# The first unit's second product in Strassen form, and all sums of the second weights made in one stage

## The chip, the cores and the metric

The kernel runs on one core of a Trainium2 chip. The metric is the device time of one execution in microseconds (us). The core has a matrix engine (TensorE, "PE" in the profile, its weight loads "PEld"), VectorE ("DVE"), ScalarE ("ACT"), GpSimd ("POOL"), and SyncE ("SP"), which here only issues transfers. Each engine works through its own list of instructions in order, and waits at an instruction until what it needs has been signalled by the others.

## The reference

Attention over chunks of 64 tokens, then a layer norm and a two-layer FFN with a residual:

```python
scores = scale * np.matmul(q_c, k_c.transpose(0, 1, 2, 4, 3))   # 8 x 8 heads, chunks of 64, D = 64
attn = softmax(scores)                                          # max subtracted
x = np.matmul(attn, v_c)                                        # -> (8, 576, 512) = 4608 tokens x 512
xn = (x - mu) / np.sqrt(var + 1e-06) * g_ln
ch = np.maximum(xn @ w_ch1, 0.0) @ w_ch2                        # 512 -> 2048 -> 512
return x + ch
```

All of it is float32. The kernel gets that accuracy from the matrix engine's faster float32 format by splitting each operand into a high and a low part and adding three products: high by high, high by low, low by high.

## The kernel before

The 4608 tokens are nine tiles of 512, each of two pairs of 256. The first three tiles (numbers 0, 1 and 2) go through the FFN in the plain way: for each of 16 blocks `f` of 128 hidden features, `up(f)` is 12 matmuls into one of two PSUM banks called `h` (line L565), `split(f)` makes the high part `hh` on ScalarE (L578) and the low part `hl` on VectorE (L579), and `down(f)` is 12 matmuls into the four banks `y` (L589): eight that read `hh`, then four that read `hl`. A bank `h` is free again when `hl` has been made.

The other six tiles form three units of two tiles (1024 tokens). In a unit both products can go by a Strassen scheme: seven products of half the size in each direction, on sums of the operand's quarters, in place of eight. The first product does so in all units (`product`, L1049, 336 matmuls of 512 columns). The second does so in units 1 and 2 (class `double`, L960, 672 matmuls of 256 columns each); in unit 0 it is plain (L1175, 384 matmuls of 512 columns). The weights stream from DRAM through a ring of six buffers.

The Strassen form needs sums of the second weights' quarters, in high and low parts, for eight pairs `p` of 128-row blocks. `mix` makes one of the eight: two adds of 128x512 (L992), four additions or subtractions of 128x256 (L999), one cast of 128x1024 on ScalarE (L1002), two subtractions of 128x512 (L1005), and two writes of 512 KB into the DRAM tensor `wb` (L1009, L1010). `mix_early` does it from the weights that are still in the local memory, during the third tile's FFN: numbers 4, 5 and 6 on GpSimd, number 7 on VectorE from the end of that stage into unit 0. `mix_late` does numbers 0 to 3 on VectorE at the end of unit 0, from ring buffers.

While the FFN of one tile or unit runs, the attention of later ones runs beside it. Its matmuls are scores (`s`, L309) and attention by values (L409). In most pairs the latter writes two banks `h`, the same two that `up` uses; VectorE then divides out of both (L443) and frees them. Between the two, a turned copy of the probabilities is made, on VectorE (`STREAM_TRANSPOSE`, L380) or on the matrix engine (L358, L368).

The order of all this is written by hand. For the first three tiles it is a table of letters per step (`START`, `SECOND`, `THIRD`): each letter advances one generator by one `yield`, ahead of the FFN's step of that number. In `THIRD`, which belongs to the third tile's FFN (number 2), `C`, `D`, `G`, `H` are attention, `S` writes the first weights' sums, `T`, `V`, `W` are the mixing of numbers 4 and 5, 6, and 7, and `P`, `Q` are `combine`, which makes unit 0's operands `xc` (casts on ScalarE L798, differences `rows` on VectorE L805, low parts on GpSimd L802). For units, `BEGINS`, `PAIR_STEPS`, `HALVES` give the counts of matmuls at which the next unit's generators advance. SyncE's list follows the same order, so a transfer there waits behind every one that was written ahead of it.

Of the kernel before, what the change touches and what calls it, by code (L numbers as in the profile page):

```python
# [17 lines left out]
P = 128  # L18
# [33 lines left out]
BEGINS = ((8, 122, 236, 350), (4, 92, 154, 246))  # L52
STEPS = (0, 5, 9, 14, 20, 31, 42, 53, 61, 67, 72, 77, 85, 90, 97, 104, 116, 128, 140)
ACROSS = (0, 5, 9, 14, 20, 31, 42, 53, 61, 67, 72, 77, 110, 116, 123, 130, 142, 154, 166)
# [28 lines left out]
FAST = 1  # L83
# [24 lines left out]
def chunk_attention_ffn(ctx: ExitStack, tc: tile.TileContext, qkv, v01, g, w, out):  # L108
# [598 lines left out]
    class Ring:  # L707
# [313 lines left out]
    def mix_late(i):  # L1021
        first = ring.passed + 4 * i

        def parts_of(k):
            w = ring.at(first + k)[:, : 2 * DM].rearrange("p (h n) -> p h n", h=2).bitcast(F32)
            return w[:, 0], w[:, 1]

        return mix(i, shared[f"h{2 * i}"][:, 0], shared[f"h{2 * i + 1}"][:, 0].bitcast(F32R), parts_of, nc.vector)

    def unit_ffn(u):  # L1030
        first = 2 * LEAD + 4 * u
        fast = u >= FAST
# [48 lines left out]
        plan = double(u, hu, mix_2, mix_3, mix_4) if fast else None  # L1081

        more = []
        order = [(n, f) for n in range(2) for f in order_of(u, n)]
        parts = []

        def split(i):
            n, f = order[i]
            if i % 5 > 1:
                hh, hl = more[i % 5 - 2][:, 0], more[i % 5 - 2][:, 1]  # L1090
            else:
                hh, hl = (hp_.tile([P, 1, DM], F32R, name=f"h{c}")[:, 0] for c in "hl")
            x = hu[f // 2][:, n, f % 2]
            nc.scalar.activation(hh, x, AF.Relu)
            parts.append((hh, hl, x))

        def rest(i):
            hh, hl, x = parts[i]
            nc.vector.scalar_tensor_tensor(
                out=hl, in0=x, scalar=0.0, in1=hh.bitcast(F32), op0=ALU.max, op1=ALU.subtract  # L1100
            )

        for q in range(NF // 4):
# [25 lines left out]
            for e in range(2):  # L1129
                steps += [  # L1130
                    (a_, e, "4", lambda e: nc.scalar.activation(h[e][:, 0, 1], a_[e], AF.Relu if fast else AF.Copy))
                ]
            for i, (bank, e, name, then) in enumerate(steps):
                if i % 2 == 0:
                    w01 = pair_of()
                product(bank[e], w01[i % 2], name, name in "215")
                yield 6
                if i % 2:
                    ring.fetch()
                if then:  # L1140
                    then(e)
                if fast:
                    if name == "7":
                        waiting.append((14 * q + i + 2, h[e][:, 1, 1]))
                    if waiting and waiting[0][0] <= 14 * q + i:
                        relu(waiting.pop(0)[1])
                    if q > 0 and i in (4, 6):
                        mix_1(2 * (q - 1) + i // 2 - 2)
                    if q == NF // 4 - 1:
                        plan.advance((i + 1 - len(steps)) * 0.945)  # L1150
                    if q == NF // 4 - 1 and i in (12, 13):
                        mix_1(2 * q + i - 12)
                    continue
                if q == NF // 4 - 1 and name in "73":
                    (split if name == "7" else rest)(e)
                if q == NF // 4 - 1 and name == "4":
                    if e == 0:
                        for n, g in ((2, "raw"), (1, "wf")):
                            x = raws.tile([P, n, 2, DM], F32R, name="hx", tag=g)
                            more.extend(x[:, i] for i in range(n))  # L1160
                    (rest if e else split)(2)

        if fast:
            assert not waiting
            yield from plan.products()
            return
# [180 lines left out]
```

## Time and profile before

| | us |
|---|---|
| median of three runs (lowest, highest) | 831.44 (830.99, 833.67) |
| the profiled execution | 830.98 |
| its span, first to last instruction | 829.2 |
| busy: TensorE / VectorE / ScalarE / GpSimd | 819.8 / 602.8 / 326.8 / 174.3 |
| unit 0 (from its first matmul to unit 1's) | 325.7 to 499.5 |
| unit 1 | 499.5 to 668.6 |

A row of the timeline has the start, the length, the engine, the line, the operation, its output and inputs, the number of instructions that are merged in it, and in brackets how long its engine sat idle ahead of it and who ended that. A merged row's length runs from the first start to the last end. In the chain of waits a row has start, length and the engine's work. In a table of stages each engine has its busy time and in brackets its number of instructions.

### The profile page before, as it was taken

What the parts mean: (1) busy time and instruction counts of PE and PEld (TensorE: products, weight loads), DVE (VectorE), ACT (ScalarE), POOL (GpSimd) and SP (SyncE); (2) the same over time, 40 slices, a digit from 0 to 9 for tenths busy, and PEclk for the clock granted to TensorE, in tenths of its full rate; (3) what the DMA queues carried; (4) which work ended last, traced back from release to release, by engine and by line L of the source; (5) the groups of instructions that cost most, each with busy time, mean ns of one, the idle gap of its engine ahead of it and who ended that gap; (6) DMA issues with size and microseconds to landing.
All of it is one profiled execution on the core that took longest, in us unless ns stands there. A gap on an engine that the chain in (4) does not pass through costs nothing.

```text
span 829.2 us, 16241 instructions
## 1 busy us (share of the span) xinstructions
PE 819.8 (99%) x6442; PEld 701.1 (85%) x6442; DVE 602.8 (73%) x983; ACT 326.8 (39%) x513; POOL 174.3 (21%) x156
## 2 busy tenths in 40 slices
PE   7999999999999999999999999999999999999998
PEld 5898888888888887888888888888999988889998
DVE  6998966787655956876787866797889953248954
ACT  4776431132332332323324433434544632354432
POOL 0110006463855754000005101000002700000000
PEclk9999999999999999999999999999999999999999
DMA  9998416958784336978877999787796686668662
GB/s 360 331 279 238 157 47 222 344 172 291 282 294 125 128 136 254 326 223 301 266 245 214 347 300 346 263 262 249 246 308 211 181 285 196 195 190 286 212 209 104
DMA packets 105531, 199.53 MB, mean 241 GB/s; under 512 B 8816, under 2 KB 61552, under 8 KB 103536
## 3 DMA queue, kind: packets, MB, share of 16 engines
q1 hardware_dynamic: 103008, 191.68, 68.0%
q0 software_dynamic: 2448, 6.82, 4.4%
q8 instruction: 51, 0.84, 0.4%
q14 instruction: 24, 0.20, 0.1%
HBM read 140.79 MB, written 48.76 MB: 229 GB/s over the span
## 4 chain that ended last, share of the span: by engine, by line
PE 98%; DMA 1%; DVE 0%; SPq 0%; issue 0%; ACT 0%; DVEq 0%
PE y L1049 28%; PE y L960 19%; PE h L565 16%; PE y L589 16%; PE y L1175 8%; PE h L1175 3%; PE s L309 2%; PE h L409 1%; DMA k_t<-qkv 1%; PE s L409 1%; PE s L358 1%; PE s L335 0%; PE y L249 0%; PE s L497 0%; PE y L518 0%; PE s L518 0%
## 5 line engine op out<-in xcount | busy, mean ns | idle before, releaser
L1049 PE MATMUL y<-xc,ring 128*128 128x512 f32 x1008 | 233.7, 391 | 0.0
L1049 PEld LDWEIGHTS y<-xc,ring 128*128 128x128 f32 x1008 | 187.9, 188 | 39.5
L565 PE MATMUL h<-xth,wp 128*128 128x512 f32 (+1 forms) x432 | 129.5, 370 | 0.0
L960 PE MATMUL y<-ring,hx 128*128 128x256 f32 x876 | 108.5, 283 | 0.0
L960 PEld LDWEIGHTS y<-ring,hx 128*128 128x128 f32 x876 | 106.6, 192 | 0.0
L1058 DVE TENSOR_TENSOR hu<-y,snap 128x512 f32<-128x512 f32 x72 | 49.1, 687 | 67.1 <-ACT snap L1055 35.0
L589 PE MATMUL y<-wp,hh 128*128 128x512 f32 x376 | 96.2, 394 | 0.0
L565 PEld LDWEIGHTS h<-xth,wp 128*128 128x128 f32 x432 | 78.2, 188 | 14.4 <-DVE hl L579 0.5
L589 PEld LDWEIGHTS y<-wp,hh 128*128 128x128 f32 x376 | 69.1, 188 | 13.9
L579 DVE SCALAR_TENSOR_TENSOR hl<-h,hh 128x512 fp32r<-128x512 f32 (+1 forms) x53 | 33.1, 629 | 62.4 <-ACT hh L578 62.0
L565 PE MATMUL h<-xtl,wp 128*128 128x512 f32 (+1 forms) x216 | 78.3, 367 | 0.0
L1055 ACT COPY snap<-y 128x512 f32<-128x512 f32 x72 | 42.0, 586 | 79.2 <-PE y L1049 79.2
L578 ACT ACTIVATE hh<-h 128x512 fp32r<-128x512 f32 (+1 forms) x53 | 28.7, 546 | 105.7 <-PE h L565 105.7
L380 DVE STREAM_TRANSPOSE pt_sb<-p_sb 32x256 f32<-32x256 f32 x144 | 62.7, 436 | 4.6 <-ACT p_sb L344 2.3
L802 POOL TENSOR_TENSOR xc<-rows,xc 128x512 fp32r<-128x512 f32 x28 | 49.8, 1788 | 73.8 <-ACT xc L798 72.2
L897 ACT ACTIVATE hx<-hu 128x512 fp32r<-128x512 f32 x73 | 45.3, 630 | 49.1 <-PE y L960 44.3
L906 DVE TENSOR_TENSOR hx<-hu,hx 128x512 fp32r<-128x512 f32 x62 | 45.3, 740 | 11.6 <-ACT hx L897 10.9
L459 POOL TENSOR_TENSOR rstd<-vare,mhalf 128x2 f32<-128x2 f32 x12 | 11.1, 927 | 194.8 <-DVE vare L458 194.8
L589 PE MATMUL y<-wp,hl 128*128 128x512 f32 x188 | 51.8, 390 | 0.0
L565 PEld LDWEIGHTS h<-xtl,wp 128*128 128x128 f32 x216 | 40.3, 188 | 6.6 <-ACT xtl L528 0.2
L960 PE MATMUL y<-ring,hh 128*128 128x256 f32 x312 | 45.2, 283 | 0.0
L1175 PE MATMUL y<-ring,hx 128*128 128x512 f32 x162 | 42.2, 390 | 0.0
(168 smaller groups left out, 1197.2 us busy)
## 6 DMA issues: line engine op xcount, KB each, us to landing
ring<-wa SPq DMA_DIRECT2D x84, 512.0 KB, 4.6
ring<-w2d SPq DMA_DIRECT2D x56, 512.0 KB, 5.0
ring<-wb SPq DMA_DIRECT2D x32, 512.0 KB, 4.0
raw<-w SPq DMA_DIRECT2D x15, 1024.0 KB, 8.0
out<-x SPq DMA_DIRECT2D x18, 512.0 KB, 5.3
q_t<-qkv SPq DMA_DIRECT2D x17, 512.0 KB, 5.8
k_t<-qkv SPq DMA_DIRECT2D x17, 512.0 KB, 6.7
v_t<-qkv SPq DMA_DIRECT2D x32, 256.0 KB, 6.1
```

The source lines that it names most:

```text
L380: nc.vector.transpose(out=pt_sb[quad(2 * h2 + j), :, c, quad(i)], in_=p_sb[quad(2 * c + i), :, h2, quad(j)])
L565: nc.tensor.matmul(h, lhsT=(wh, wh, wl)[m][:, ks], rhs=(xth, xtl, xth)[m][:, k, :], start=i == 0, stop=i == len(terms) - 1,)
L579: nc.vector.scalar_tensor_tensor(out=hl, in0=h, scalar=0.0, in1=hh.bitcast(F32), op0=ALU.max, op1=ALU.subtract)
L589: nc.tensor.matmul(sums(pairs[j // 2])[j % 2], lhsT=(hh, hh, hl)[m], rhs=(wh, wl, wh)[m], start=f == 0 and m == 0, stop=f == NF - 1 and m ...
L802: engine.tensor_tensor(out=o[:, 1], in0=x, in1=o[:, 0].bitcast(F32), op=ALU.subtract)
L897: nc.scalar.activation(hh, self.split[i][2], AF.Relu if x == "1" else AF.Copy)
L906: nc.vector.tensor_tensor(out=hl, in0=x, in1=hh.bitcast(F32), op=ALU.subtract)
L960: nc.tensor.matmul(bank[j // 2][:, j % 2 * PAIR : (j % 2 + 1) * PAIR], lhsT=(hh, hh, hl)[m][:, j * P : (j + 1) * P], rhs=loaded[t // 2][:, ...
L1049: nc.tensor.matmul(bank, lhsT=w[:, (0, 0, 1)[m], ks], rhs=x[:, (0, 1, 0)[m], k, :], start=start and k == m == 0, stop=k == 1 and m == 2, s ...
L1055: nc.scalar.copy(out, bank)
L1058: nc.vector.tensor_tensor(out=out, in0=bank, in1=s, op=ALU.add)
L1175: nc.tensor.matmul(ys[j], lhsT=(hh, hh, hl)[m], rhs=w[:, (0, 1, 0)[m]], start=f == 0 and m == 0, stop=f == NF - 1 and m == 2,)
```

## The change

Unit 0's second product takes the Strassen form too, so that all units have one plan; the plain code, its table entries and `mix_late` go. The sums of the second weights must then all be in DRAM by unit 0's second product. All eight are made in the third tile's stage: 4, 5, 6 on GpSimd as before, and 1, 2, 3, 7 and 0 on VectorE. Numbers 1, 2, 3 and 7 are made from the weights in local memory, in the places `w1`, `w2`, `w3`, `w8`; number 0's weights have gone by then, and are read back from DRAM into `w9` (`mix_again`).

```diff
 THIRD = {
-    ... 6: "DGS", 7: "GGHSTT", 8: "DGTT", 9: "D", 10: "GGPT",
+    ... 6: "DGSaa", 7: "GGHSTTaa", 8: "DGTTabb", 9: "Daaabb", 10: "GGPTcc", ...
...
-BEGINS = ((8, 122, 236, 350), (4, 92, 154, 246))
+BEGINS = (4, 92, 154, 246)
...
-PAIR_STEPS = ((STEPS, STEPS, ACROSS, STEPS), (STEPS, BY_TENSOR, WIDE, AT_END))
-HALVES = (((426, 8), (562, 12)), ((512, 8), (612, 10)))
+PAIR_STEPS = (STEPS, BY_TENSOR, WIDE, AT_END)
+HALVES = ((512, 8), (612, 10))
...
-            ring.loads.extend(w2d[f][:, :, :] for n in range(2) for f in order_of(u, n))
-            continue
...
-    def mix_late(i):
...
-        return mix(i, shared[f"h{2 * i}"][:, 0], shared[f"h{2 * i + 1}"][:, 0].bitcast(F32R), parts_of, nc.vector)
+    def mix_again(tag, p):
+        t_ = const.tile([P, 2, 2, DM], F32, name="mixed", tag=tag)
+        for k in range(2):
+            nc.sync.dma_start(t_[:, :, k], w2d[2 * p + k])
+        yield
+        yield from mix(
+            p, t_[:, 0], t_[:, 1].bitcast(F32R), lambda k: [t_[:, 0, k], t_[:, 1, k]], nc.vector
+        )
...
-        plan = double(u, hu, mix_2, mix_3, mix_4) if fast else None
+        plan = double(u, hu, mix_2, mix_3, mix_4)
...
-                nc.scalar.copy(staged[:, jj], ys[j])
-                nc.gpsimd.dma_start(spilled[pair][:, jj], staged[:, jj], accum_op=ALU.add)
...
-            V=mix_early(const, "w7", (6,), nc.gpsimd), W=mix_early(const, "w12", (7,), nc.vector), ...
+            V=mix_early(const, "w7", (6,), nc.gpsimd), W=mix_early(const, "w8", (7,), nc.vector), ...
+            a=mix_early(const, "w1", (1,), nc.vector), b=mix_early(const, "w2", (2,), nc.vector), c=mix_early(const, "w3", (3,), nc.vector),
+            d=mix_again("w9", 0), P=combine(0, 0), Q=combine(0, 1),
...
-                by_pe = len(PAIR_STEPS[u - 1][n]) == len(BY_TENSOR)
+                by_pe = len(PAIR_STEPS[n]) == len(BY_TENSOR)
...
-        side = [(at, now["Q"]) for at in REST] + [(at, now["W"]) for at in LAST_MIXED]
+        side = [(at, now["Q"]) for at in REST]
```

The lines of the changed file are numbered lower: L579 becomes L574, L443 L438, L409 L404, L992 L975, L999 L982, L1005 L988, L960 L943, L724 L719.

VectorE's list in the third tile, from the low part of block 5 to the attention division of the pair on letter `G`. Before:

```order
L579 SCALAR_TENSOR_TENSOR hl<-h,hh 128x512 x2
L380 STREAM_TRANSPOSE pt_sb<-p_sb 32x8x32 x16
L579 SCALAR_TENSOR_TENSOR hl<-h,hh 128x512
L387 TENSOR_REDUCE den<-p_sb 128x16
L388 TENSOR_SCALAR den<-den 128x16
L389 RECIPROCAL rden<-den 128x16
L443 TENSOR_TENSOR x<-h,rden 128x8x64 x2
```

The first row holds the low parts of blocks 4 and 5, the third that of block 6. In the changed kernel the same stretch, from the end of number 2's (`b`) quarters on, reads:

```order
L982 TENSOR_TENSOR mixed<-mixed 128x256 x4
L574 SCALAR_TENSOR_TENSOR hl<-h,hh 128x512
L375 STREAM_TRANSPOSE pt_sb<-p_sb 32x8x32 x8
L975 TENSOR_TENSOR mixed<-wp 128x512 x2
L375 STREAM_TRANSPOSE pt_sb<-p_sb 32x8x32 x8
L982 TENSOR_TENSOR mixed<-mixed 128x256 x4
L574 SCALAR_TENSOR_TENSOR hl<-h,hh 128x512
L382 TENSOR_REDUCE den<-p_sb 128x16
L383 TENSOR_SCALAR den<-den 128x16
L384 RECIPROCAL rden<-den 128x16
L988 TENSOR_TENSOR mixed<-mixed 128x512 x2
L438 TENSOR_TENSOR x<-h,rden 128x8x64 x2
```

Between the low parts of blocks 5 and 6 now stand number 3's (`c`) two adds and four quarter operations, and ahead of the division number 2's two subtractions.

SyncE's list from the end of the third tile into unit 0. Before:

```order
L1009 DMA wb<-mixed 128x1024
L1010 DMA wb<-mixed 128x1024
L724 DMA ring<-wa 128x1024 x2
L268 DMA x<-out 128x2x512 x2
L281 DMA q_t<-qkv 128x1024
L281 DMA k_t<-qkv 128x1024
L724 DMA ring<-wa 128x1024 x4
L612 DMA out<-x 128x512 x4
```

In the changed kernel:

```order
L719 DMA ring<-wa 128x1024 x2
L992 DMA wb<-mixed 128x1024
L993 DMA wb<-mixed 128x1024
L263 DMA x<-out 128x2x512 x2
L276 DMA q_t<-qkv 128x1024
L276 DMA k_t<-qkv 128x1024
L719 DMA ring<-wa 128x1024 x4
L992 DMA wb<-mixed 128x1024
L993 DMA wb<-mixed 128x1024
L607 DMA out<-x 128x512 x4
```

Number 7's writes now stand ahead of the loads of `x` (the third tile's residual), of the next pair's q and k, and of four ring buffers; number 0's stand behind them.

TensorE's list at the start of unit 0. Before:

```order
L1049 MATMUL y<-xc,ring 128x512 x12
L309 MATMUL s<-k_t,q_t 64x64 x32
L1049 MATMUL y<-xc,ring 128x512 x66
L409 MATMUL h<-v_t,pt_sb 64x64 x32
L1049 MATMUL y<-xc,ring 128x512 x48
```

In the changed kernel:

```order
L1031 MATMUL y<-xc,ring 128x512 x6
L304 MATMUL s<-k_t,q_t 64x64 x32
L1031 MATMUL y<-xc,ring 128x512 x66
L404 MATMUL h<-v_t,pt_sb 64x64 x32
L1031 MATMUL y<-xc,ring 128x512 x24
L304 MATMUL s<-k_t,q_t 64x64 x32
L1031 MATMUL y<-xc,ring 128x512 x30
L363 MATMUL s<-ident,p_sb 128x128 x8
```

The scores come six matmuls earlier, the next pair's follow sooner, and two of the four pairs are turned on the matrix engine (L363), as in unit 1 before. Within the third tile TensorE's list is the same as before.

More of the change, by code (lines that the diff above doesn't have):

```diff
@@ L82 @@
 LONG = 40
-FAST = 1
 def layout(room, side, tail=False):
@@ L1154, in unit_ffn @@
[L1154 to L1166, printed above, removed]
@@ new lines, in unit_ffn @@
+                if name == "7":
+                    waiting.append((14 * q + i + 2, h[e][:, 1, 1]))
+                if waiting and waiting[0][0] <= 14 * q + i:
+                    relu(waiting.pop(0)[1])
+                if q > 0 and i in (4, 6):
+                    mix_1(2 * (q - 1) + i // 2 - 2)
+                if q == NF // 4 - 1:
+                    plan.advance((i + 1 - len(steps)) * 0.945)
+                    if i in (12, 13):
+                        mix_1(2 * q + i - 12)
+        assert not waiting
@@ L1220, in weave @@
+        yield from plan.products()
     def weave(ffn, side):
@@ L1287, in chunk_attention_ffn @@
         now["N"] = following(1, 0)
-        now.update(zip("u1", tiles[2].ffn(0, 2, room=ROOMS[2])), X=bring(range(2 * LEAD - 2, 2 * LEAD)))
+        now.update(zip("u1", tiles[2].ffn(0, 2, room=ROOMS[2])))
         play(layout(ROOMS[2], THIRD, True), now)
-        side = [(at, now["Q"]) for at in REST] + [(at, now["W"]) for at in LAST_MIXED]
+        side = [(at, now["Q"]) for at in REST]
         for u in range(UNITS):
@@ L1293, in chunk_attention_ffn @@
                 for n in range(4):
-                    begin, steps = BEGINS[u][n], PAIR_STEPS[u][n]
+                    begin, steps = BEGINS[n], PAIR_STEPS[n]
                     side += [(begin + at, following(u + 1, n)) for at in steps]
                     side.append((begin + steps[0], following(u + 1, n + 1)))
-                for half, (begin, step) in enumerate(HALVES[u]):
+                for half, (begin, step) in enumerate(HALVES):
                     stream = combine(u + 1, half)
                     side += [(begin + i * step, stream) for i in range(13)]
-            if u + 1 == FAST:
-                starts = {}
-                def late(i):
-                    if i not in starts:
-                        starts[i] = mix_late(i)
-                    next(starts[i])
-                for i in range(NF // 4):
-                    side += [(SECOND_HALF + 12 * i * 4 + at, calls(late, i)) for at in MIXING]
             side = weave(unit_ffn(u), side)
```

108 lines of the change are left out of this document (7 added, 101 removed).

## The prediction

> **What bounds the kernel now.** I read the page's busy times and the shares of the chain that ended last, then the stages by windows, then the timeline of single engines where the change puts new work.
>
> ```profile
> PE 819.8 (99%) x6442; PEld 701.1 (85%) x6442; DVE 602.8 (73%) x983; ACT 326.8 (39%) x513; POOL 174.3 (21%) x156
> PE 98%; DMA 1%; DVE 0%; SPq 0%; issue 0%; ACT 0%; DVEq 0%
> ```
>
> The matrix engine is the whole path: 98% of the chain. Removing matmuls shortens the kernel, and any wait that the change puts on that engine lengthens it, one for one. The stages (busy time and count of each engine):
>
> ```profile
> 325.70:499.50 173.80, 173.80 (x1234) 142.68 (x1233) 135.46 (x231) 61.33 (x102) 20.83 (x19) 1.00 0.84 274
> 499.50:668.60 169.10, 169.10 (x1538) 152.88 (x1537) 142.67 (x229) 77.43 (x130) 25.39 (x13) 1.00 0.79 256
> 255.00:272.00 17.00, 17.00 (x195) 13.76 (x194) 11.29 (x24) 4.08 (x7) 10.51 (x10) 1.00 0.24 94
> 272.00:300.00 28.00, 28.00 (x187) 23.15 (x186) 26.37 (x45) 10.69 (x17) 20.91 (x20) 1.00 0.30 114
> ```
>
> Units 0 and 1 (first two rows) keep the matrix engine busy without a gap. Unit 1 already runs the plan that unit 0 is to get, with 84% of VectorE's time (142.67 of 169.10), and still without a gap. The last two rows are parts of the third tile's stage. From 272 to 300 VectorE is busy for 26.37 of 28 us and GpSimd for 20.91: there is no room for more work on VectorE there, unless something may come later.
>
> **Unit 0.** In the chain of waits (start, length, work):
>
> ```profile
> 325.71 2.72 PE y L1049 x12
> 532.02 0.87 PE s L368 x8
> 573.56 0.87 PE s L368 x8
> 588.01 80.63 PE y L960 x672
> 496.78 2.72 PE h L1175 x12
> ```
>
> 384 plain matmuls at 2.72/12 = 0.227 us make 87.0 us. The 672 that replace them take 80.63 in unit 1. That is 6.4 us less, not an eighth, since 256 columns cost 0.120 us each. Two pairs more are turned on the matrix engine, 2 x 0.87 = 1.7 us more. Together -4.7 us, the difference of the first two windows too. I take -4.7. Unit 0's other changes I cost at nothing: VectorE's and ScalarE's splits, and loading and storing `x` on SyncE in place of GpSimd's accumulating transfers, all do the same in unit 1 behind full TensorE time, which is the cover. Were VectorE the bound, the four mixings that leave the end of unit 0 would be a gain; under a full matrix engine they bring nothing.
>
> **The mixing, moved into the third tile.** Prices are in these rows:
>
> ```profile
> 317.30 1.28 DVE L992 TENSOR_TENSOR mixed<-wp 128x512 f32<-128x512 f32 x2
> 319.11 0.87 DVE L999 TENSOR_TENSOR mixed<-mixed 128x256 f32<-128x256 f32 x2
> 330.88 0.68 DVE L1005 TENSOR_TENSOR mixed<-mixed 128x512 fp32r<-128x512 f32 x1
> ```
>
> One mixing costs VectorE 1.28 + 2 x 0.87 + 2 x 0.68 = 4.4 us. Whether it costs time depends on the place:
>
> ```profile
> 253.82 0.69 DVE L579 SCALAR_TENSOR_TENSOR hl<-h,hh 128x512 fp32r<-128x512 f32 x1 [3.75 <-ACT hh L578]
> 260.25 0.69 DVE L579 SCALAR_TENSOR_TENSOR hl<-h,hh 128x512 fp32r<-128x512 f32 x1 [5.74 <-ACT hh L578]
> 260.86 7.21 DVE L380 STREAM_TRANSPOSE pt_sb<-p_sb 32x256 f32<-32x256 f32 x16
> 268.10 0.69 DVE L579 SCALAR_TENSOR_TENSOR hl<-h,hh 128x512 fp32r<-128x512 f32 x1
> 270.50 1.29 DVE L443 TENSOR_TENSOR x<-h,rden 128x512 f32<-128x512 f32 x2
> 276.57 0.68 DVE L579 SCALAR_TENSOR_TENSOR hl<-h,hh 128x512 fp32r<-128x512 f32 x1
> ...
> 303.19 0.69 DVE L579 SCALAR_TENSOR_TENSOR hl<-h,hh 128x512 fp32r<-128x512 f32 x1 [2.79 <-ACT hh L578]
> 309.56 0.69 DVE L579 SCALAR_TENSOR_TENSOR hl<-h,hh 128x512 fp32r<-128x512 f32 x1 [5.68 <-ACT hh L578]
> ```
>
> These are the low parts of blocks 4 to 7, and of 12 and 13, with the turning and the division between. The order puts number 1 whole and number 2's adds and quarters ahead of block 5's low part: 4.4 + 3.0 = 7.4 us, against 3.75 + 5.74 = 9.5 us of idle time. Nothing. Numbers 7 and 0 fall into the gaps at the stage's end, 8.8 us against 2.79 + 5.68 and the 3.0 that number 7 already took there: nothing either. ScalarE's cast for each mixing finds it busy for 4.08 of 17 and 10.69 of 28 us. The operands `xc` will lie where numbers 1, 2 and 3 were mixed, so their casts wait for those writes; number 1's is issued ahead of block 5's low part, its cast stands behind it: nothing.
>
> Number 3 stands behind 260.25, where VectorE has no idle time up to block 6's low part, and that one is on the path already:
>
> ```profile
> 268.93 1.02 PEld L409 LDWEIGHTS h<-v_t,pt_sb 64*64 64x64 f32 x64 [0.35 <-DVE hl L579]
> 272.88 0.39 PE L565 MATMUL h<-xth,wp 128*128 128x512 f32 x1
> 280.13 1.07 PE L589 MATMUL y<-wp,hl 128*128 128x512 f32 x4
> ```
>
> Attention by values (L409) needs both banks `h`, of blocks 5 and 6, and waited 0.35 us for block 6's low part. Number 3's two adds and four quarters, 1.28 + 1.74 = 3.0 us, come ahead of that low part, so everything behind L409 on TensorE's list (block 5's and 6's `down`, the next `up`) is 3.0 us late. That is firm. What is late next: the division (L443), which frees the banks for the `up` at 272.88, has number 2's two subtractions (1.36) ahead of it. Its first half ended near 271.2, so by durations alone it ends at 271.2 + 3.0 + 1.4 = 275.6, under the 275.9 at which the `up` now comes. Block 7's low part gets 1.36 more: 277.3 + 5.7 = 283.0, against 283.1 needed. So the plain sum is a wait of 3.0 us, with no margin left; 3.0 to 3.6.
>
> The plain sum leaves GpSimd out, which mixes and subtracts at the same time:
>
> ```profile
> 258.13 2.55 POOL L992 TENSOR_TENSOR mixed<-wp 128x512 f32<-128x512 f32 x2 [9.23 <-DMA wa<-parts]
> 260.63 3.18 POOL L999 TENSOR_TENSOR mixed<-mixed 128x256 f32<-128x256 f32 x4
> 263.77 1.31 POOL L802 TENSOR_TENSOR xc<-rows,xc 128x512 fp32r<-128x512 f32 x1
> 265.49 1.29 POOL L802 TENSOR_TENSOR xc<-rows,xc 128x512 fp32r<-128x512 f32 x1 [0.41 <-ACT xc L798]
> 266.74 2.54 POOL L1005 TENSOR_TENSOR mixed<-mixed 128x512 fp32r<-128x512 f32 x2
> 272.05 2.55 POOL L992 TENSOR_TENSOR mixed<-wp 128x512 f32<-128x512 f32 x2 [2.76 <-DMA wb<-mixed]
> 284.08 3.00 POOL L1005 TENSOR_TENSOR mixed<-mixed 128x512 fp32r<-128x512 f32 x2
> 280.11 0.68 DVE L805 TENSOR_TENSOR rows<-rows 128x512 f32<-128x512 f32 x1
> 284.16 1.75 DVE L805 TENSOR_TENSOR rows<-rows 128x512 f32<-128x512 f32 x1 [1.05 <-POOL xc L802]
> ```
>
> The same VectorE operation takes 0.68 us at 280.11, where GpSimd is idle, and 1.75 at 284.16, where GpSimd's started 0.08 ahead; GpSimd's pair took 3.00 instead of 2.54. It waited out about one GpSimd operation, 1.07 us. The mixing's operations are of the same kind, two inputs from the local memory. Eight of them (2 adds, 4 quarters, 2 subtractions) stand ahead of the division. Lower end: none meets GpSimd, 0. Upper end: each loses 1.07, 8.6 us. I walk it through. Number 2's quarters meet the adds of 258.13: +0.5, first transposes to 265.0. Number 3's first add meets the tail of the operation at 263.77 (0.4), its second the whole of the next (1.3): 268.0 with their own 1.3. Second transposes to 271.6; quarters 1.7 and 0.3 for the tail of 266.74's pair; low part 0.7: 274.3, and L409 starts 5.4 us late. The three small rows of the denominator take 1.8, and 0.6 for one that meets the adds of 272.05 (themselves moved to 274); number 2's subtractions 1.4 and 0.7; first half of the division 0.65: 279.5. The `up` of 272.88 comes at 279.6. So the wait is 6.7 us, within 3.0 to 11.6; I take 6.7, since GpSimd is busy for 62 and 75% of the two windows. Block 7's low part then ends near 286, needed at 286.8.
>
> By the Trainium skill, SBUF — State Buffer, section "Who interferes with whom", a VectorE instruction with two SBUF inputs contends with a GpSimd instruction that reads SBUF, and the second to issue "fully blocks" until the first ends. The row at 284.16 agrees (1.07 us). By that rule the sum comes out as here, near 6.7; with GpSimd left out it would be 3.0.
>
> **Sum.** -4.7 + 6.7 = +2.0 us on the profiled execution's 830.98: 833.0. The median lies 0.46 above that execution: 833.4.
>
> **Rivals.**
>
> GpSimd costs nothing: only the plain 3.0 to 3.6 us. For it: the row at 280.11, undisturbed at 0.68. -4.7 + 3.3 = -1.4: 830.0.
>
> The wait is covered: if ScalarE's `hh` or the first `up` came later anyway, number 3 would be hidden. Against it: L409 already waited for that low part. 831.4 - 4.7 = 826.7.
>
> On the slow side, a matrix engine that sits still loses speed:
>
> ```profile
> 2.39 6.11 PE L249 MATMUL y<-minus 128*128 128x512 f32 x14 [2.39 <-ACT minus L1270]
> 14.87 1.16 PE L309 MATMUL s<-qk_b 64*64 64x64 f32 x64 [1.11 <-ACT p_sb L339]
> ```
>
> Its first 14 matmuls, after idleness, took 6.11/14 = 0.44 us instead of 0.227. After 1.11 us of idleness it was not seen slower. The change makes one wait of some 5.4 us in one piece. If the engine then runs at half speed for 6.1 us, that is 3.0 us, of which 1.3 pass while it waits for the division anyway: +1.7 to 3, 835.2. It decides where the wait at L409 outlasts the idle time that the engine bears, somewhere above 1.11 us. The Trainium skill, TensorE: Matmul & The Clock Gate, section "What's actually happening", says that one idle window of about 3.4 us halves the clock; a 5.4 us wait can hold one, a 3.0 us wait cannot. No row here shows a wait of that length.
>
> Also slow: the seam into unit 0.
>
> ```profile
> 303.47 0.32 SPq L1010 DMA_DIRECT2D wb<-mixed  x1
> 307.01 0.94 SPq L268 DMA_DIRECT2D x<-out  x2
> 317.08 1.75 SPq L724 DMA_DIRECT2D ring<-wa  x4
> 317.00:327.00 10.00, 10.00 (x44) 7.71 (x43) 8.14 (x16) 3.20 (x5) 5.31 (x5) 1.00 0.78 289
> ```
>
> GpSimd's last write (number 6, 303.47) may slip by several us; the two ring loads behind it are wanted at 325.7, so that is covered. But `x`, q and k, issued from 307.01 on, now stand behind number 7's write. That waits for VectorE's subtractions, some 5 us behind the low part at 309.56, so they go at 315, 8 us later, next to four ring loads: 5 MB with the write, 17 us at the 289 GB/s of the last row. The third ring load is wanted 2 x 2.72 + 1.1 us into unit 0, 17 us after. If number 0's write shares the time, 3 us are lost: 836.4. That decides where the transfers run below 290 GB/s.
>
> **How the numbers follow.** A difference under 0.3%, 2.5 us, is about what cannot be told from none: 828.9 to 833.9. Forecast (833.4, alone 831.7 to 835.0, waits of 5.0 to 8.3 us): 0.47, of which 0.28 lies under 833.9. Plain sum, 830.0: 0.20. Covered, 826.7: 0.06. Clock, 835.2: 0.17. Seam, 836.4: 0.10. Faster 0.06; same 0.20 + 0.28 = 0.48; slower 0.19 + 0.17 + 0.10 = 0.46. The range reaches from just below the plain sum to just above the seam: 829.8 to 836.6.
>
> **What would show it.** Unit 0 should last 169.1 us like unit 1. L404 (the old L409) on the bank `h` near 269 should wait 5 to 6 us for the low part at L574, and the `up` behind it for the division (L438); rows of L975 and L982 on VectorE should exceed 0.68 and 0.42 us, and GpSimd's in the same stretch their 1.29. If these are undisturbed, the plain sum holds. Matmuls 0.44 us apart behind the wait would show the clock, and waits for ring loads at the start of unit 0 the seam. If L404 waits under 2 us, my reading of VectorE's list is wrong.

## The result, and the profile after

The changed kernel takes 839.85 us in the median of four runs (838.76 to 840.30), the kernel before 831.62 (830.99 to 833.67): a ratio of 1.0093, with a 95% interval of 1.0073 to 1.0113. It is slower by 8.2 us, where +2.0 was forecast, and outside the range that was given. The profiled execution took 839.96 us with a span of 838.0.

The lines of the page that answer to those of before, busy time of each engine, the clock by slices and the shares of the chain that ended last:

```profile
PE 818.5 (98%) x6746; PEld 713.6 (85%) x6746; DVE 643.5 (77%) x1023; ACT 345.8 (41%) x545; POOL 179.3 (21%) x148
PEclk9999999999999799999999999999999999999999
PE 89%; DVE 7%; DMA 2%; ACT 1%; issue 1%; SPq 0%; DVEq 0%; ACTq 0%
```

VectorE had 0% of the chain and now has 7%, some 60 us, of which 20.7 lie between 257 and 279 us, in the third tile's stage. (The rest lies at the kernel's start, at the stage's end and in unit 1, where the matrix engine's waits are short.) One slice of forty has a granted clock of 7, at that same place. The stages by windows (start and end, length, busy time of PE, PEld, DVE, ACT and POOL, the clock, the DMA's share, GB/s), two calls of the view, units 0 and 1 first:

```profile
338.20:507.40 169.20, 169.20 (x1538) 152.99 (x1537) 144.01 (x231) 77.21 (x130) 25.45 (x12) 1.00 0.80 266
507.40:677.20 169.80, 169.64 (x1538) 153.00 (x1537) 146.44 (x235) 77.21 (x130) 23.95 (x11) 1.00 0.77 255
...
269.80:278.30 8.50, 0.38 (x5) 0.19 (x4) 8.26 (x15) 0.62 (x1) 5.55 (x5) 0.73 0.30 123
278.30:285.00 6.70, 6.70 (x74) 5.59 (x75) 6.49 (x13) 0.42 (x1) 1.93 (x3) 0.58 0.43 154
285.00:300.00 15.00, 15.00 (x110) 12.36 (x111) 13.18 (x20) 7.53 (x12) 6.46 (x6) 1.00 0.44 175
```

Unit 0 lasts 169.2 us where it lasted 173.8, as forecast. But from 269.8 to 278.3 the matrix engine does nothing for 8 us, and in the 6.7 us behind that its mean clock is 0.58 (half speed until 283.9, full behind it). The timeline of the matrix engine, and then of VectorE and GpSimd, at that place (start, length, the work, in brackets the idle time ahead of it and what ended it):

```profile
269.85 0.33 PE L404 MATMUL h<-v_t,pt_sb 64*64 64x64 f32 x4
278.30 1.97 PE L404 MATMUL h<-v_t,pt_sb 64*64 64x64 f32 x60 [8.12 <-DVE hl L574]
280.20 3.78 PE L584 MATMUL y<-wp,hh 128*128 128x512 f32 x8
```

```profile
253.27 1.79 DVE L982 TENSOR_TENSOR mixed<-mixed 128x256 f32<-128x256 f32 x4
...
258.32 4.16 DVE L982 TENSOR_TENSOR mixed<-mixed 128x256 f32<-128x256 f32 x4
262.40 0.68 DVE L574 SCALAR_TENSOR_TENSOR hl<-h,hh 128x512 fp32r<-128x512 f32 x1
263.00 3.58 DVE L375 STREAM_TRANSPOSE pt_sb<-p_sb 32x256 f32<-32x256 f32 x8
266.61 3.30 DVE L975 TENSOR_TENSOR mixed<-wp 128x512 f32<-128x512 f32 x2
269.93 3.60 DVE L375 STREAM_TRANSPOSE pt_sb<-p_sb 32x256 f32<-32x256 f32 x8
273.56 4.09 DVE L982 TENSOR_TENSOR mixed<-mixed 128x256 f32<-128x256 f32 x4
277.57 0.68 DVE L574 SCALAR_TENSOR_TENSOR hl<-h,hh 128x512 fp32r<-128x512 f32 x1
...
280.08 1.22 DVE L988 TENSOR_TENSOR mixed<-mixed 128x512 fp32r<-128x512 f32 x2
```

```profile
258.43 2.88 POOL L975 TENSOR_TENSOR mixed<-wp 128x512 f32<-128x512 f32 x2 [8.63 <-DMA wa<-parts]
261.28 3.41 POOL L982 TENSOR_TENSOR mixed<-mixed 128x256 f32<-128x256 f32 x4
267.62 3.42 POOL L988 TENSOR_TENSOR mixed<-mixed 128x512 fp32r<-128x512 f32 x2
273.84 2.66 POOL L975 TENSOR_TENSOR mixed<-wp 128x512 f32<-128x512 f32 x2 [2.81 <-DMA wb<-mixed]
```

L404 stands for block 6's low part, which ends at 278.25. Ahead of it VectorE does number 2's quarters (4.16 us), number 3's adds (3.30) and number 3's quarters (4.09), each beside a GpSimd row. Number 1's quarters at 253.27, ahead of GpSimd's first row, took 1.79. L404 and the first eight `down` matmuls behind it then take 1.97 and 3.78 us, where 1.16 and 2.11 were needed before.

All the code ahead of the attention by values near 237 us is the same in every kernel here, and yet it starts between 236.4 and 240.7 us from profile to profile. So the table gives, from the starts of rows in each trace, the stage (that attention row to unit 0's first matmul), unit 0 (to unit 1's first matmul) and the rest, in us:

| kernel | that row | stage | unit 0 | rest |
|---|---|---|---|---|
| before | 236.8 | 88.8 | 173.8 | 329.8 |
| after | 237.7 | 100.5 | 169.1 | 330.6 |
| number 3 from DRAM in unit 0 | 238.5 | 90.7 | 174.7 | 330.5 |
| number 3 behind the division | 240.6 | 100.4 | 170.2 | 330.5 |
| dummy matmuls | 236.6 | 97.8 | 169.1 | 330.6 |
| GpSimd's mixings away | 237.8 | 95.2 | 184.9 | 330.7 |
| GpSimd's mixings later | 238.9 | 99.7 | 170.1 | 330.6 |
| the same, wait half filled | 237.7 | 99.7 | 169.8 | 330.6 |
| number 3 away, GpSimd later | 240.7 | 92.2 | 173.3 | 330.5 |
| number 3 away, stores sooner | 236.4 | 90.3 | 175.2 | 330.5 |
| number 3 on GpSimd | 237.1 | 91.8 | 170.2 | 330.6 |
| number 3's arithmetic left out | 237.7 | 92.8 | 169.1 | 330.6 |
| number 3 on GpSimd, subtractions behind | 237.6 | 89.4 | 169.2 | 330.6 |

In the two executions that come to that row last (240.6 and 240.7) the matrix engine had waited 2.3 us for a load of weights near 50 us and run at half speed for 3.4 us behind it.

From before to after, then: +0.9 ahead of the stage (which differs between executions anyway), +11.8 in the stage, -4.7 in unit 0, +0.8 behind it; 8.8 us, the difference of the spans.

### The profile page after: what moved, and what is told of

Same layout as the page of the kernel before. It is cut to its first block, busy times and chain, and to the rows that moved or that the text cites. A ratio compares the mean times of both kernels' runs of the same rounds, so it can differ in the third digit from the quotient of the medians.

```text
span 838.0 us, 16961 instructions
## 1 busy us (share of the span) xinstructions
PE 818.5 (98%) x6746; PEld 713.6 (85%) x6746; DVE 643.5 (77%) x1023; ACT 345.8 (41%) x545; POOL 179.3 (21%) x148
## 4 chain that ended last, share of the span: by engine, by line
PE 89%; DVE 7%; DMA 2%; ACT 1%; issue 1%; SPq 0%; DVEq 0%; ACTq 0%
PE y L943 29%; PE y L1031 26%; PE y L584 14%; PE h L560 14%; PE s L304 2%; DVE pt_sb L375 2%; PE h L404 1%; DVE mixed L982 1%; DMA wp<-wfs 1%; DMA k_t<-qkv 1%; PE s L404 1%; PE s L330 0%; PE s L363 0%; PE s L353 0%; DVE mixed L975 0%
## 5 line engine op out<-in xcount | busy, mean ns | idle before, releaser
L943 PE MATMUL y<-ring,hx 128*128 128x256 f32 x1272 | 158.0, 283 | 0.0
L943 PEld LDWEIGHTS y<-ring,hx 128*128 128x128 f32 x1272 | 155.0, 192 | 0.0
L584 PE MATMUL y<-wp,hh 128*128 128x512 f32 x376 | 97.9, 399 | 0.0
L880 ACT ACTIVATE hx<-hu 128x512 fp32r<-128x512 f32 x106 | 65.8, 630 | 65.8 <-PE y L943 60.9
L785 POOL TENSOR_TENSOR xc<-rows,xc 128x512 fp32r<-128x512 f32 x28 | 60.5, 2173 | 128.8 <-ACT xc L781 127.2
L889 DVE TENSOR_TENSOR hx<-hu,hx 128x512 fp32r<-128x512 f32 x90 | 67.4, 758 | 15.1 <-ACT hx L880 13.2
L943 PE MATMUL y<-ring,hh 128*128 128x256 f32 x496 | 71.8, 283 | 0.0
L574 DVE SCALAR_TENSOR_TENSOR hl<-h,hh 128x512 fp32r<-128x512 f32 (+1 forms) x53 | 32.9, 627 | 45.8 <-ACT hh L573 45.4
L943 PEld LDWEIGHTS y<-ring,hh 128*128 128x128 f32 x496 | 65.2, 192 | 0.2
L880 ACT ACTIVATE hh<-hu 128x512 fp32r<-128x512 f32 x62 | 38.8, 631 | 31.6 <-PE y L943 29.1
L375 DVE STREAM_TRANSPOSE pt_sb<-p_sb 32x256 f32<-32x256 f32 x112 | 48.8, 436 | 3.6 <-ACT p_sb L339 1.7
```

The source lines that it names most:

```text
L375: nc.vector.transpose(out=pt_sb[quad(2 * h2 + j), :, c, quad(i)], in_=p_sb[quad(2 * c + i), :, h2, quad(j)])
L574: nc.vector.scalar_tensor_tensor(out=hl, in0=h, scalar=0.0, in1=hh.bitcast(F32), op0=ALU.max, op1=ALU.subtract)
L584: nc.tensor.matmul(sums(pairs[j // 2])[j % 2], lhsT=(hh, hh, hl)[m], rhs=(wh, wl, wh)[m], start=f == 0 and m == 0, stop=f == NF - 1 and m ...
L785: engine.tensor_tensor(out=o[:, 1], in0=x, in1=o[:, 0].bitcast(F32), op=ALU.subtract)
L880: nc.scalar.activation(hh, self.split[i][2], AF.Relu if x == "1" else AF.Copy)
L889: nc.vector.tensor_tensor(out=hl, in0=x, in1=hh.bitcast(F32), op=ALU.subtract)
```

## The experiments

All start from the changed kernel. Their lines are shifted a little: L401, L405 and L408 are the attention by values, L571, L575 and L578 the low parts, L972 and L976 the mixing's adds, L979 its quarters, L985 its subtractions, L982 its cast, L581 and L585 `down`, L557 `up`, L435 the division. Each comparison is with runs of the kernel before on the same chip.

### Number 3 taken out of the stage

```diff
-c=mix_early(const, "w3", (3,), nc.vector)      # tokens 10 to 15 of THIRD
+c=mix_late(("h6",), (3,), nc.gpsimd)           # from DRAM, unit 0, steps at 100, 116, ... 228
```

> Number 3 alone is taken out of the third tile's stage: its two blocks are read back from DRAM and mixed on GpSimd in unit 0's first product, where its buffer (the fourth column set's first) is free for 57 us. All else as in the changed kernel. Theory (number 3's adds and quarters, lengthened by GpSimd, stand before block 6's hl, and the long wait also halves the matrix engine's clock): the wait of L404 falls from 8.3 us to under 0.8, no slice of the span has a clock under 9, and unit 0 starts about 10.6 us earlier than in the changed kernel; 7.9 + 2.7 us are given back, span 827.4, time 829 (828 to 830.5). Rival, the seam: the loads at unit 0's start are what is late and unit 0 starts late anyway, time 834 or more. Rival, VectorE is short of time in the whole stage: the wait only moves to a later operand of the attention, 832 or more.

It took 836.45 us, 1.0052 of before (1.0033 to 1.0071). The stage gave back 9.8 of its 11.8 us, and no clock was lost there, so the long wait is number 3's place. But unit 0 lost 5.6 us. The timeline of the matrix engine in its first product, and the windows around it (whose DMA share is the last but one number):

```profile
410.87 1.43 PE L401 MATMUL h<-v_t,pt_sb 64*64 64x64 f32 x49 [3.71 <-DMA v_t<-qkv]
```

```profile
404.00:411.00 7.00, 3.29 (x24) 2.49 (x26) 2.89 (x6) 2.47 (x5) 0.00 (x0) 1.00 1.03 411
411.00:413.00 2.00, 2.00 (x65) 1.79 (x64) 0.30 (x1) 0.00 (x0) 0.00 (x0) 0.64 0.95 289
```

Number 3 adds 2 MB of transfers to that product, 1 MB read and 1 MB written. Its stores went out at 396.5 us, beside the next pair's loads, while the DMA engines were busy all the time, and v_t was 3.7 us late; the clock fell behind that wait too. That it was the stores, and not the reads, is argued here and not shown; in the changed kernel the DMA share from 404 to 411 us is 1.00 as well, without a wait. That part of the expectation was a miss: the seam wasn't late, a place inside unit 0 was.

### Number 3 behind what waits

```diff
-10: "GGPTcc", 11: "HGGPTTbcc", 13: "GTTbc", 14: "GGHPcc", 15: "GHPTc",
-c=mix_early(const, "w3", (3,), nc.vector)
+c=mix_early(const, "w4", (3,), nc.vector)
+15: "GHPTcc", 16: "GHPTTc", 17: "GPTVVc", 18: "HHGPVVc", 19: "HGPc", 20: "HGPVcc",
```

> The same work at the same engine, but number 3's eight pieces are played at tokens 15 to 20 instead of 10 to 15, so that they stand behind block 6's hl and the attention's division, in another buffer. Theory: L404's wait falls below 0.8 us and the clock stays, but VectorE is 94% busy from 272 to 300 us in the changed kernel and the attention's next operands have 1 to 1.5 us of slack there, so 6 to 8 us of mixing come out as new waits of 2 to 5 us in sum behind it: 831 to 834. Rival, only the place mattered and the rest is covered: 829. Rival, the amount of work in the stage decides and not its place: 838 or more.

It took 838.93 us, 1.0091 (1.0070 to 1.0113). L401's wait fell to 1.35, and a wait of 4.7 us came at the turning of the layer norm's rows (L489), which waits for ScalarE's scaling and so for VectorE's late division and sums; the eight matmuls behind it took 3.76:

```profile
274.39 1.15 PE L401 MATMUL h<-v_t,pt_sb 64*64 64x64 f32 x60 [1.35 <-DVE hl L571]
279.75 0.50 PE L557 MATMUL h<-xth,wp 128*128 128x512 f32 x1 [1.27 <-DVE x L435]
...
314.14 1.11 PE L489 MATMUL s<-ident,xg 128*128 128x128 f32 x4 [4.67 <-ACT xg L463]
314.91 3.76 PE L581 MATMUL y<-wp,hh 128*128 128x512 f32 x8
```

The stage is as long as in the changed kernel (100.4 for 100.5). VectorE has no room there, and the wait moved, as the theory said; but it was under-priced (1.35 + 1.27 + 4.67 us of waits instead of 2 to 5, and the clock fell with the last of them), and the time lies where the rival had put it that the amount of work decides and not its place (838 or more). The run doesn't separate the two. Its profile is of the slowest of six executions (843.60 us), so these sizes may be at the upper end.

### The clock

```diff
+            if pair == 2 * LEAD + 1:
+                for _ in range(30):
+                    nc.tensor.matmul(o[0], lhsT=minus, rhs=wide, start=True, stop=True)
```

> Thirty matmuls of 128x128 on 128x512 are written into the attention output's own first bank just before L404, whose results the real ones overwrite; at 0.23 us each they fill 6.8 us of the 8.3 us that the matrix engine waits there, and nothing waits for them. Theory of the clock (the wait itself drops it): the granted clock stays at full in this stage, L404 takes 1.1 us instead of 1.97 and the 12 matmuls behind it 2.9 instead of 4.65, so the time falls by 2.7 us to 837.1. Rival, the clock dropped for another reason (or the lower clock costs nothing): 839.9, the two durations as in the changed kernel. Rival, the dummies hold up the real ones: over 840.5.

It took 836.57 us, 1.0052 (1.0037 to 1.0068), 3.3 under the changed kernel; the stage is 2.7 shorter.

```profile
268.68 6.96 PE L395 MATMUL h<-minus 128*128 128x512 f32 x30
275.58 0.33 PE L408 MATMUL h<-v_t,pt_sb 64*64 64x64 f32 x4
277.04 1.15 PE L408 MATMUL h<-v_t,pt_sb 64*64 64x64 f32 x60 [1.13 <-DVE hl L578]
278.12 2.12 PE L588 MATMUL y<-wp,hh 128*128 128x512 f32 x8
```

The low part comes no earlier, and 30 useless matmuls fill the time until then. The real ones behind take 1.15 and 2.12 us instead of 1.97 and 3.78. The wait itself dropped the clock, and that was worth 2.7 us.

### GpSimd's mixings taken away

```diff
-T=mix_early(raws, "raw", (4, 5), nc.gpsimd), V=mix_early(const, "w7", (6,), nc.gpsimd)
+T=mix_late(("h6", "h7", "h6"), (4, 5, 6), nc.gpsimd)      # from DRAM, in unit 0's first product
```

> GpSimd's three mixings (numbers 4, 5 and 6) are taken out of the stage and done from DRAM in unit 0's first product; VectorE's mixings stay where the change put them. Theory of contention (GpSimd's streams lengthen VectorE's): number 2's quarters take 1.8 us instead of 4.16, number 3's adds 1.3 instead of 3.3 and its quarters 1.8 instead of 4.09, so L404 waits 1 to 3.4 us instead of 8.3, which is what the adds and quarters of number 3 take by themselves plus what was there before; without a drop of the clock the time is 831 to 832.5, with a drop like the one of the changed kernel 833.5 to 835. Rival, the quarters are slow for another reason (DMA, or the operation itself in this stage): they keep 4.1 us, the wait stays above 7, 839 or more. Rival: the three mixings' loads and stores make unit 0's first product wait for its weights: over 835 with waits for ring tiles.

VectorE's rows at the same place, and the matrix engine's:

```profile
258.40 1.80 DVE L979 TENSOR_TENSOR mixed<-mixed 128x256 f32<-128x256 f32 x4
261.25 0.69 DVE L571 SCALAR_TENSOR_TENSOR hl<-h,hh 128x512 fp32r<-128x512 f32 x1 [1.05 <-ACT hh L570]
...
265.47 1.29 DVE L972 TENSOR_TENSOR mixed<-wp 128x512 f32<-128x512 f32 x2
...
270.40 1.80 DVE L979 TENSOR_TENSOR mixed<-mixed 128x256 f32<-128x256 f32 x4
```

```profile
272.86 1.97 PE L401 MATMUL h<-v_t,pt_sb 64*64 64x64 f32 x60 [2.60 <-DVE hl L571]
274.76 3.78 PE L581 MATMUL y<-wp,hh 128*128 128x512 f32 x8
```

The three groups take 1.80, 1.29 and 1.80 us instead of 4.16, 3.30 and 4.09: 6.7 us of the changed kernel are GpSimd's lengthening. Here 1.05 us of that is idle time ahead of block 5's low part, and about the rest shows in the wait, which falls from 8.1 to 2.6. What is left is number 3's own two adds and four quarters. The clock fell with 2.6 us as it did with 8.1. (GpSimd's stores and ScalarE's casts of the three mixings left the stage too; the next run keeps them in it.) The kernel as a whole took 848.43 us, 1.0198 (1.0183 to 1.0214), since the three mixings in unit 0 made its first product wait (4.5 us for a ring tile, 4.3 for VectorE's sums): unit 0 is 15.8 us longer. That was the second rival, and larger than put.

### GpSimd's mixings moved back, and the wait half filled

```diff
 # letters T and V only
-7: "..TT", 8: "..TT", 10: "T", 11: "TT", 12: "TTT", 13: "TT", 15: "T", 16: "TT", 17: "TVV", 18: "VV", 20: "V", 21: "VV", 22: "V"
+12: "TT", 13: "TT", ... 19: "TT", 20: "VV", 21: "V", 22: "VV", 23: "V", 24: "VV"
```

> The changed kernel with one thing moved: GpSimd's mixings of numbers 4 and 5 begin at token 12 instead of 7 and number 6's at token 20 instead of 17, so that they no longer run beside VectorE's adds and quarters of numbers 2 and 3; all work stays in the stage. Theory (5.7 of the 8.3 us at L404 are GpSimd's lengthening, 2.6 are number 3's own adds and quarters): VectorE's quarters go back to 1.8 us and the adds to 1.3, L404 waits 2.6 to 3 us, and since the clock fell after 2.6 us in the run without GpSimd, it falls here too (L404 1.97 us): 834 (833 to 835.5), 5.7 below the changed kernel. Rival, GpSimd then meets VectorE's later rows (subtractions, the sums L788) and the attention's next operands come late: waits of 1 to 4 us behind the division, 835.5 to 838. Rival, GpSimd ends later and unit 0's operands are late: a wait at unit 0's start.

It took 839.36 us, 1.0087 (1.0075 to 1.0099). Number 2's and number 3's quarters, which no longer meet a GpSimd row, took 1.79 and 1.80 us again, with all the work still in the stage: what lengthens them is GpSimd's rows beside them. L401's wait was 3.7 us (number 3's adds still met a GpSimd row, 2.39 us), and 2.8 us of a new one came, at L489 again: ScalarE's list is in order, and its cast of number 6 stood there waiting 4.45 us for GpSimd's late quarters, ahead of the copies that the matrix engine needed:

```profile
314.07 1.04 ACT L982 CAST mixed<-mixed 128x1024 fp32r<-128x1024 f32 x1 [4.45 <-POOL mixed L979]
315.02 0.59 ACT L570 ACTIVATE hh<-h 128x512 fp32r<-128x512 f32 x1
315.51 0.58 ACT L490 COPY rows<-s 128x512 f32<-128x512 f32 x1
```

The first rival came nearest, though by another engine than the one it named, and its 835.5 to 838 was too low. With eight dummy matmuls as well:

> The kernel of the run before (GpSimd's mixings later) with eight dummy matmuls before L404, 1.9 us, which leave 0.7 us of its wait. Theory: waits of 0.35 to 1.35 us left the clock alone in four traces and 2.6 us dropped it, so here it stays full; L404 takes 1.15 us and the twelve matmuls behind it 3.2: 2.7 us less than the run before, 831.4 (830 to 833), level with the kernel before the change. Rival, below 3 us of wait the clock's drop costs less than in the changed kernel: 0 to 1.5 us less than the run before.

It took 839.88 us, 1.0092 (1.0079 to 1.0105): nothing gained, and the expectation missed. Of the 3.7 us the dummies filled 1.98 and left 1.88:

```profile
269.75 1.98 PE L392 MATMUL h<-minus 128*128 128x512 f32 x8
271.65 0.33 PE L405 MATMUL h<-v_t,pt_sb 64*64 64x64 f32 x4
273.87 1.30 PE L405 MATMUL h<-v_t,pt_sb 64*64 64x64 f32 x60 [1.88 <-DVE hl L575]
275.09 3.51 PE L585 MATMUL y<-wp,hh 128*128 128x512 f32 x8
```

The clock fell with 1.88 us too (3.51 instead of 2.11). In the trace's own windows, 3.41 us each:

```profile
271.31:274.73 3.42, 1.54 (x62) 1.06 (x62) 3.29 (x7) 1.49 (x2) 0.00 (x0) 1.00 0.00 0
274.73:278.14 3.41, 3.41 (x24) 2.71 (x16) 3.31 (x8) 0.51 (x1) 0.00 (x0) 0.50 0.22 92
```

All of the wait lies in the first window, where the matrix engine is busy for 1.54 us; the whole of the next runs at half speed.

### Both moved, and the stores sooner

```diff
+[(at, now["c"]) for at in (100, 104, 108, 116, 124, 140, 156, 164, 200)]      # stores at 200 instead of 228
```

> Number 3 is mixed from DRAM by GpSimd in unit 0's first product as in the first run, but with its steps closer together and its two stores at 200 units of the walk instead of 228, before the next pair's q, k and v are called for; and GpSimd's mixings of 4, 5 and 6 begin later as above. Theory: L404 waits under 0.5 us, the clock stays, the wait of 3.7 us for v_t in unit 0 goes, the seam costs at most 0.7 us: span 827, time 828.5 (827 to 830), faster than the kernel before by 3. Rival, the megabyte of stores takes time from unit 0's loads wherever it stands: a wait for v_t, k_t or a ring tile of 2 to 5 us remains and the time is 831 to 835. Rival, GpSimd's later mixings make unit 0's operands late: a wait at its start.

837.22 us, 1.0057 (1.0045 to 1.0069). The stage is 92.2 us, with 2.4 at L489 behind the same cast; unit 0 is 4.1 longer than in the changed kernel, with 2.0 for v_t and 0.9 for a ring tile. So the rival of the stores came nearest, though its 831 to 835 was too low. Neither the wait at L489 nor the one for v_t dropped the clock, though both are longer than 1.88 us:

```profile
312.06 0.66 PE L489 MATMUL s<-ident,xg 128*128 128x128 f32 x4 [2.44 <-ACT rows L490]
```

```profile
307.60:311.02 3.42, 2.02 (x9) 1.31 (x7) 0.00 (x0) 1.03 (x2) 2.28 (x3) 1.00 0.00 0
311.02:314.43 3.41, 2.37 (x13) 2.03 (x14) 2.80 (x4) 1.57 (x4) 2.70 (x2) 1.00 0.37 154
```

Here the wait falls into two windows, 1.40 us into the first and 1.04 into the second, and the clock stays full. Without moving GpSimd's mixings:

> Number 3 from DRAM in unit 0 with the closer steps and earlier stores, GpSimd's other mixings where the change put them. Against the first run only the steps differ: by the theory that its stores (issued at 396 us, beside the loads of the next pair) made v_t 3.7 us late, that wait goes and the time falls from 836.4 by 4 to 5.5 us to 831.5 (830 to 833), with L404's 0.9 us left. Rival, the stores are in the way at any place: 834.5 to 837.

835.01 us, 1.0042 (1.0025 to 1.0060). Unit 0 still loses 6.1 us (1.8 for v_t, 0.7 for a ring tile, 0.8 for ScalarE, and a clock of 0.62 in the 3 us from 411). The stores went out 61.1 us into unit 0 instead of 67.2 (387.86 and 396.46 by SyncE's timeline), which halved the wait for v_t and brought others. The rival held: at neither place had unit 0's first product room for another 2 MB.

### Number 3 on GpSimd, in its gaps

```diff
-c=mix_early(const, "w3", (3,), nc.vector)      # 10: cc, 11: cc, 13: c, 14: cc, 15: c
+c=mix_early(const, "w4", (3,), nc.gpsimd)      # 12: cc ahead of T, 15: cc, 16: c, 18: cc ahead of V, 19: c
-V: 17: VV, 18: VV, 20: V, 21: VV, 22: V
+V: 17: VV, 18: VV, 23: V, 24: VV, 26: V
```

> Number 3 stays in the third tile's stage and is mixed from SBUF, but on GpSimd, in its gaps: its adds while GpSimd waits for number 4's store, its quarters behind the attention's power (rstd), its subtractions ahead of number 6's quarters; number 6's cast on ScalarE is played later, behind the two copies of the turned rows, so that ScalarE's queue doesn't stand behind GpSimd. No megabyte is added to unit 0's loads. Theory: L404 waits under 1 us, the clock stays, unit 0's first product has no new wait; the stage is 1.5 to 2.5 us longer than before the change, unit 0 4.65 shorter, unit 1 0.7 longer: 829.5 to 831, by 1 to 2.5 us faster than the kernel before. Rival, some operand that stands behind a mixing on GpSimd's or ScalarE's queue comes late (the power, the turned rows, unit 0's operands): a wait of 2 to 4 us and the half clock after it, 832 to 836.

831.37 us, 0.9994 (0.9981 to 1.0007): 8.5 us under the changed kernel and level with the one before. L401 waits 0.41 and no clock is lost. One wait of 1.2 us stands behind it, since number 2's two subtractions meet a GpSimd row just ahead of the division:

```profile
271.47 3.21 DVE L985 TENSOR_TENSOR mixed<-mixed 128x512 fp32r<-128x512 f32 x2
274.60 1.28 DVE L435 TENSOR_TENSOR x<-h,rden 128x512 f32<-128x512 f32 x2
```

```profile
275.34 0.50 PE L557 MATMUL h<-xth,wp 128*128 128x512 f32 x1 [1.22 <-DVE x L435]
```

Unit 0 is 1.1 us longer than in the changed kernel, with 0.8 of waits for v_t, though no transfer was added to it.

### The floor: number 3's arithmetic left out

```diff
+        for q in [p, 3] if p == 2 else [p]:      # number 2's results are stored for number 3 too
```

> Number 3's arithmetic is left out: number 2's results are stored in its place too, so the stores and the later loads are the same and the ten operations on VectorE and ScalarE are gone (the result is then another). It is the floor: what the change would give if number 3 were mixed at no cost. Theory: L404's wait under 1 us, no drop of the clock, span 827 to 828 and time 829 to 830, 10 below the changed kernel; about 10.6 of its 8.2 lost and 2.4 hidden gains are then number 3's place. Rival, other parts of the change cost too: 832 or more with waits elsewhere.

832.07 us, 0.9993 (0.9978 to 1.0008), 7.8 under the changed kernel. It was the more telling miss: without number 3 the change still gains nothing. The stage is 4.0 us longer than before it, with 1.37 at L401 (number 2's quarters take 4.71 us beside GpSimd's rows), 1.26 at the `up` behind the division, and 0.7 at the last `down` matmuls, which wait for ScalarE's last relu, behind a cast that waits for VectorE.

### Two pairs of subtractions moved behind what waits for them

```diff
-12: "ccGTTTbb", 13: "GTTb", 14: "GGHP", 15: "GHPTcc", 29: "QXXNdd", 30: "QQRd", 31: "Q"
+12: "ccGTTT", 13: "GTT", 14: "GGHPbb", 15: "GHPTccb", 29: "QXXN", 30: "QQR", 31: "Qddd"
```

> The last kernel with number 3 on GpSimd, and two of VectorE's pieces moved behind what is waited for: number 2's two subtractions (3.21 us there, beside GpSimd's stream) from ahead of the attention's division to behind the sums that follow it, and number 0's two subtractions from ahead of the last rows' sum to behind the stage's last hl. Theory (in that kernel the matrix engine waits 1.2 us at `up` for the division and 0.7 us at the stage's end for ScalarE's last relu, which stands behind a cast that waits for that sum): both waits go, 1.9 us less: 829.5 (828.5 to 831), faster than the kernel before by 0.3%. Rival, the subtractions then make the next hl or the rows of the turned tile late, and the waits only move: 831 to 833.

829.71 us, 0.9978 (0.9966 to 0.9991): faster than the kernel before by 0.2%, and by 10.1 us than the changed one, as expected (829.5). From 200 to 510 us the matrix engine has one wait left:

```profile
PE h L401 <- DVE hl L571: 0.4, 1, 0.4
```

The stage is 0.6 us longer than before the change, unit 0 4.6 shorter. Of unit 0's 4.6 us about 2 reach the median. It is the only kernel of the study whose interval lies below 1, but only just, and it is the best of eleven that were tried: the 10 us against the changed kernel are sure, the 0.2% is at the edge of what these runs can tell.

## Why the prediction was wrong

- **Unit 0, -4.7 us: right.** 173.8 to 169.1 us by starts of rows. That the rest of unit 0 costs nothing was nearly right: the part behind it is 0.8 us longer, of which 0.6 is a wait for VectorE's `hu` early in unit 1.
- **Numbers 1, 2, 7 and 0 at nothing: wrong.** The step compared durations with idle time and left GpSimd to a later step, in which number 2's quarters delayed what stands behind them by 0.5. They took 2.4 longer (4.16 for 1.80); 1.05 us of idle time covered a part, and 1.3 came through. With number 3's arithmetic gone, these four still cost 4.0 us of the stage; with number 3 on GpSimd and two pairs of subtractions moved, 0.6.
- **Number 3's own work, 3.0 us: right.** Without GpSimd's mixings L401 waited 2.60 us, and its sixty matmuls started 2.8 us later than before, counted from the row near 237 us.
- **GpSimd's lengthening, the term that was mis-sized, and the step that failed.** The walk took +2.4 us up to L404 (its 5.4 less the firm 3.0); it was some 5.5 (8.1 less 2.6). Number 3's adds were forecast well (+1.7, measured 2.0). Its quarters were given 0.3 and lost 2.3: GpSimd's next adds, which the walk had put behind them, came at 273.84, 0.28 us after the quarters had begun. The walk had the quarters at 271.6 and those adds at 274; on its clock (this execution runs 0.9 us later) they came at 272.7 and 272.9. A microsecond in either list decides whether such rows meet. The upper end of the step, every operation losing 1.07, allowed it; the walk's single value was given too much trust. The Trainium skill, SBUF — State Buffer, section "Who interferes with whom", says that two SBUF inputs on VectorE contend with a GpSimd instruction that reads SBUF. The runs agree: the same rows take 1.80 and 1.29 us without GpSimd's mixings beside them. The words "fully blocks" that the prediction quotes stand there in the line on VectorE's two-port modes; the section's rule that the shared port pair is an exclusive lock covers both.
- **The division, +1.3 us: absent in the changed kernel, present elsewhere.** The walk let number 2's subtractions meet a GpSimd row. In the changed kernel GpSimd's quarters had ended before they began, they took 1.22 us, and the `up` didn't wait; with the dummy matmuls, at full clock, it was the same. In three kernels they met one, took 3.21 or 3.22 us, and the `up` waited 1.22 to 1.27.
- **The clock, a rival with 0.17: it came true, beside the forecast and not in its place.** It cost 2.7 us (dummy matmuls), as priced. The rival was made to exclude the forecast, though a longer wait brings both. By the window of about 3.4 us that the Trainium skill names (TensorE: Matmul & The Clock Gate, "What's actually happening") a wait of 3.0 us was taken as safe. The runs differ: waits of 1.88 and 2.60 us dropped it. Nor is there one length of wait that does: 1.97 and 2.44 us left it alone. What the traces show is a window of 3.41 us. Every stretch of half speed inside the kernels lasts 3.41, 6.83 or 10.24 us, and where a trace has several, their starts lie whole multiples of 3.413 us apart. The clock fell for the next window when the matrix engine had been idle for 1.81 us or more of one (1.81 ahead of v_t in the run with the stores sooner), and held with up to 1.42 (near 55 us, with number 3 from DRAM); the one case that doesn't fit is the end of the kernel before, 1.85 us idle behind the last matmul and no drop. Once at half speed, 0.72 us of idleness was enough to keep it there. So a wait that two windows share can pass without loss. The forecast 5.4 us could not: however it falls, one window holds at least 2.7 of it.
- **The seam, 0.10: didn't come.** No wait for a transfer stands at unit 0's start; 0.7 us at the stage's end are ScalarE's last relu.

In sum the stage's +11.8 is 8.4 us by which the sixty matmuls of L404 start later (40.61 us behind the row near 237, for 32.26 before), 2.7 of clock and 0.7 at its end. The forecast had 6.7: 5.4 for that start and 1.3 for the division.

The windows also say why the clock was low at once when the work went on after the waits of 2.6 and 8.1 us, and only some way into it after those of 1.88 and 3.7 (1.30 and 1.45 us for the sixty matmuls instead of 1.97): in the first two a new window had begun during the wait, at 272.09 and 273.64 us, in the other two 0.9 and 0.7 us behind it. What stays open is where between 1.42 and 1.85 us of idleness the boundary lies, and which of number 3's transfers made v_t late in unit 0.

## What to carry to other kernels

Before work is moved in front of an operation that the bound engine waits for, price it as if a second engine that it contends with lengthened every one of its operations; where two lists could meet within a microsecond, take the upper end and not a walk. Add to a wait of more than some 1.8 us on the matrix engine the half-speed time behind it, at least 1.7 us for one window of 3.41, in the forecast itself. A wait below some 3.6 us may escape (an estimate, twice 1.81; the longest that did was 2.44), but the windows begin at another place in every trace here. A good place for moved work is the gap of an engine whose results nobody needs soon, and each of its pieces, the cast on a third engine's list too, has to stand behind what others wait for.

## What the runs showed of the hardware

- VectorE and GpSimd lengthen each other's operations with two inputs in the local memory: four quarters of 0.45 us (1.80) became 4.16, 4.09 and 4.71, two subtractions of 1.22 became 3.21, and GpSimd's own two subtractions 3.42 instead of 2.54.
- The matrix engine's clock is set anew every 3.41 us. 1.81 us of idleness in one window halved it for the next, which costs 1.7 us; 2.44 us that two windows shared did not. Filling a wait of 8 us with useless matmuls gave 2.7 us back.
- In unit 0's first product, where the DMA engines' share is 1.0 already, a load came 3.7 us late with 2 MB of further transfers (0.8 at most without them), and the waits spread to other places when the stores were moved.
